# Attention, two-expert routing and an MLP on one core: row sums with a built-in 1e-9, the routing's noise one step later, the first loads reordered

## The chip, the cores and the metric

One core of a Trainium2 chip. The metric is the device time of one execution in microseconds. The kernel before takes 890.91 us, the median of three runs (889.0 to 891.82).

## What is computed

Three parts, one after the other, in fp32.

1. Attention with hashed buckets, for 2 batches of 8 heads with 768 positions of 64 numbers. A query sees only the keys whose six sign bits (of `q @ proj`) are the same as its own:

```python
mask = q_bucket[:, :, :, None] == k_bucket[:, :, None, :]
scores = np.where(mask, scale * q @ k^T, -1e9)
attn = np.exp(scores - max);  attn = attn / (attn.sum(-1) + 1e-9);  out = attn @ v
```

2. A mixture of 8 experts over the 1536 rows of 512 that come out: `noisy = x @ w_gate + log1p(exp(x @ w_noise)) * noise`, the two best experts per row with softmax weights, and for each `relu(x @ w1[e]) @ w2[e]`.
3. An MLP with 2048 inner columns: `h = x @ w_in`, `h * sigmoid(1.702 h) @ w_out`.

## The kernel before, in words

**The attention** (`attention`, L506) is a software pipeline of 96 steps g. One step is 128 queries of one head against all 768 keys. Six steps make a unit u: two heads j and three blocks c of 128 queries; 16 units in all. TensorE is PE in the profile, VectorE DVE, ScalarE ACT, GpSimd POOL; SP issues most DMAs. Each engine works off its instructions in program order, and the order is written out by hand. In step g the program emits:

- `a_score(g+2)` (L288): four matmuls into one of two PSUM tiles `s`; `a_soft(g+2)` on DVE: the row maximum `mx` (L300) and two small operations `sm` (L301, L302);
- `a_trans(g)` (L330): six transposes of `P` into the two PSUM tiles `p`, each half copied to SBUF by ACT or DVE (L259, L265; `copy` picks the one with less work booked so far);
- `a_exp(g+2)` (L311) on ACT: exponentials into `P`, whose row sums go into a small tile `rs` (`accum_out`);
- in some steps `a_av` (L341): `P^T` times `v` into columns 0 to 383 of the PSUM tile `av` (`self.pa`); once per unit its copy `xu`;
- then whatever the table `sched` holds for this step. `at(g, f)` puts a call there; `at_m` does the same for calls that use the one PSUM tile `m`, and moves each to a step that no other such call has.

**Closing a unit** (`a_xt`, L351, 18 calls) stands in that table. It takes the PSUM tile `m` (the last call a tile `p`) of 512 columns. DVE adds 1e-9 to the unit's row sums and writes them into columns 480 to 485 of that same tile (L371), and takes the reciprocal into the SBUF tile `rc` (L372). PE then multiplies `xu` with the gate weights into columns 384 to 479 (L376) and transposes `xu` into columns 0 to 383 (L379). DVE scales both by `rc` (L382, or L384 and L385; and L386).

**The routing** of a quarter of the rows (`r_route`, L400) is cut into small functions, `soft` to `weights`, one per step. `soft` sums the logits into columns 392 and up of the tile `av` (L420 to L422), and has ACT take Exp and Ln (L423, L424). `noisy` (L427 to L429) combines that with the noise; its operands lie in `av` as well. `top` and `index` find the two best experts. For the first two quarters a loop (L567 to L576) gives each function its step. When the slots are known POOL scatters the rows to memory (L485), six DMAs for a quarter; `f_load` (L614) then reads the first expert's rows back, and `f_tr` (L619) transposes them (L821): the mixture begins.

**The start.** `a_load(0)` (L129) issues four loads of 384 KB: q of head 0, q of head 1 and k of head 1 from SP, k of head 0 from ACT. `consts` then issues the 16 KB of `projq` from ACT (L66) and the signs `sgn` from POOL (L72). 40 dummy matmuls (L514) run meanwhile. For the first unit the splitting of q and k into high and low parts is written out: `z_q` (L210) scales q into `u1` and `u2` (L218 or L216, L219) and subtracts (L220); `z_k` (L222) does k (L229 or L227, L230); for head 0 the engines are ACT and DVE, for head 1 POOL takes most. `z_hash` (L232) multiplies q and k with `projq` (L183) and turns the result into sign rows on DVE (L245, four per head) and ACT (L247).

Of the kernel before, what the change touches and what calls it, by code (L numbers as in the profile page):

```python
# [10 lines left out]
F32 = mybir.dt.float32  # L11
# [4 lines left out]
AF = mybir.ActivationFunctionType  # L16
ALU = mybir.AluOpType
AX = mybir.AxisListType
# [3 lines left out]
B, H, S, D = 2, 8, 768, 64  # L22
# [7 lines left out]
HALF = 384  # L30
# [8 lines left out]
SCALE = 1.0 / math.sqrt(D)  # L39


class Kernel:
# [19 lines left out]
    def consts(self):  # L62
        nc, a = self.nc, self.a
        p = self.cpool
        self.projq = self.t(p, [128, 32], F32, "projq")
        nc.scalar.dma_start(self.projq, a["projq"])  # L66
        self.sc = self.t(p, [128, 2], F32, "sc")
        nc.vector.memset(self.sc, 1.0)
        nc.vector.memset(self.sc[0:64, 0:1], SCALE)
        nc.vector.memset(self.sc[64:128, 1:2], SCALE)  # L70
        self.sgn = self.t(p, [128, 1], F32, "sgn")
        nc.gpsimd.dma_start(self.sgn, a["sgn"])  # L72
        self.ident = self.t(p, [128, 128], F32, "ident")
        make_identity(nc, self.ident)
# [39 lines left out]
    def attn_pools(self, ctx):  # L114
        self.ap = self.pool("attn", ctx=ctx, side="right")
        self.ps_s = self.pool("ps_s", 2, PSUM, ctx=ctx)
        self.ps_p = self.pool("ps_p", 2, PSUM, ctx=ctx)
        self.ps_a = self.pool("ps_a", 1, PSUM, ctx=ctx)
        self.ps_m = self.pool("ps_m", 1, PSUM, ctx=ctx)
        self.pa = self.t(self.ps_a, [128, 512], F32, "av")  # L120
        self.iotp = self.pa[:, HALF:HALF + 8]
        self.raw, self.uv, self.vt, self.hb = {}, {}, {}, {}
        self.tail = 0
        self.la = self.ld = 0.0
        self.rt = {}
        self.S, self.P, self.PT, self.AV = {}, {}, {}, {}
        self.RS, self.XR, self.LG, self.sm, self.xu = {}, {}, {}, {}, {}

    def a_load(self, n):  # L129
        nc, a = self.nc, self.a  # L130
        b, p = divmod(n, 4)
        raw = {}
        for j in range(2):
            for nm in ("q", "k"):
                t = self.t(self.ap, [128, S], F32, f"raw{nm}{j}", 1)
                eng = nc.scalar if n == 0 and j == 0 and nm == "k" else nc.sync
                eng.dma_start(t, a[nm + "T"][b, 2 * p + j])
                raw[nm, j] = t
        self.raw[n] = raw

# [69 lines left out]
    def z_q(self, j, hf, eng):  # L210
        nc = self.nc
        u1, v1, u2, v2 = self.uv[0, j]
        cs = slice(hf * HALF, (hf + 1) * HALF)
        q = self.raw[0]["q", j][:, cs]
        if j == 1 and hf == 0:
            eng.tensor_scalar(u1[:, cs], q, self.sc[:, 0:1], None, op0=ALU.mult)  # L216
        else:
            nc.scalar.activation(u1[:, cs], q, AF.Copy, scale=self.sc[:, 0:1])  # L218
        nc.vector.tensor_scalar(u2[0:64, cs], q[0:64, :], SCALE, None, op0=ALU.mult)  # L219
        eng.tensor_tensor(u1[64:128, cs], q[64:128, :], u1[64:128, cs].bitcast(F32), op=ALU.subtract)  # L220

    def z_k(self, j, eng):  # L222
        nc = self.nc
        u1, v1, u2, v2 = self.uv[0, j]
        k = self.raw[0]["k", j]
        if j == 1:
            eng.tensor_scalar(v1, k, self.sc[:, 1:2], None, op0=ALU.mult)  # L227
        else:
            nc.scalar.activation(v1, k, AF.Copy, scale=self.sc[:, 1:2])  # L229
        eng.tensor_tensor(v2[0:64, :], k[0:64, :], v1[0:64, :].bitcast(F32), op=ALU.subtract)  # L230

    def z_hash(self, j):  # L232
# [59 lines left out]
    def a_soft(self, g):  # L292
        nc = self.nc
        u, s, n, qh, j, c = self.dec(g)
        ps = self.S.pop(g)
        if s == 0:
            self.RS[u] = self.t(self.ap, [128, 3, 2], F32, "rs", 4)
        mx = self.t(self.ap, [128, 1], F32, "mx", 4)
        sm = self.t(self.ap, [128, 2], F32, "sm", 4)
        nc.vector.tensor_reduce(mx, ps[:, :, :HALF], axis=AX.XY, op=ALU.max, negate=True)  # L300
        nc.vector.tensor_scalar(sm[:, 0:1], mx, BIG / 2, None, op0=ALU.is_lt)  # L301
        nc.vector.tensor_scalar(sm[:, 1:2], mx, BIG / 2, mx, op0=ALU.is_lt, op1=ALU.mult)  # L302
        self.sm[g] = (sm, ps)
        self.use(dve=1.15)

    def a_exp(self, g):
        nc = self.nc
        u, s, n, qh, j, c = self.dec(g)
        sm, ps = self.sm.pop(g)
        P = self.t(self.ap, [128, 2, HALF], F32, "P", 3)  # L310
        nc.scalar.activation(P, ps[:, :, :HALF], AF.Exp, bias=sm[:, 1:2], scale=sm[:, 0:1],  # L311
                             accum_out=self.RS[u][:, c, j:j + 1])
        self.P[g] = P
        self.use(act=1.08)

# [35 lines left out]
    def a_xt(self, u, c=None, spare=False):  # L351
        nc = self.nc
        n, qh = self.un(u)
        b, p = divmod(n, 4)
        bq = 2 * b + qh
        c0, nch = (0, 3) if c is None else (c, 1)
        xu = self.xu.pop((u, c))
        if p == 0:
            if bq == 0:
                self.pad(self.ap, 96, "pad_xr")  # L360
            if bq in (1, 2):
                self.XR[bq] = self.t(self.x0, [128, 4 * CAP], F32, "xe" + "lh"[bq - 1], 1)[:, :3 * DM].rearrange("p (i d) -> p i d", i=3)
            else:
                self.XR[bq] = self.t(self.ap, [128, 3, DM], F32, "xr", 1)
            if bq == 2:
                self.pad(self.x0, 32, "pad_x0")
            self.LG[bq] = self.t(self.ap, [128, 3, 2, 16], F32, "lg", 3)
        ps = self.t(self.ps_p, [128, 512], F32, "p") if spare else self.mt([128, 512])
        rc = self.t(self.ap, [128, 3, 2], F32, "rc", 1)[:, :nch, :]
        rp = ps[:, 480:486].rearrange("p (c j) -> p c j", j=2)[:, :nch, :]  # L370
        nc.vector.tensor_scalar(rp, self.RS[u][:, c0:c0 + nch, :], 1e-9, None, op0=ALU.add)  # L371
        nc.vector.reciprocal(rc, rp)  # L372
        pt = ps[:, 0:nch * 128].rearrange("p (c d) -> p c d", c=nch)
        pl = ps[:, 384:384 + nch * 32].rearrange("p (c j e) -> p c j e", c=nch, j=2)
        for x in range(nch):
            nc.tensor.matmul(ps[:, 384 + 32 * x:416 + 32 * x], xu[:, x * 128:(x + 1) * 128], self.wg[:, p, :],  # L376
                             start=True, stop=True)
        for x in range(nch):
            nc.tensor.transpose(pt[:, x, :], xu[:, x * 128:(x + 1) * 128], self.ident)  # L379
        lg = self.LG[bq][:, c0:c0 + nch]  # L380
        if p == 0:
            nc.vector.tensor_tensor(lg, pl, rc[:, :, :, None].to_broadcast([128, nch, 2, 16]), op=ALU.mult)  # L382
        else:
            nc.vector.tensor_tensor(pl, pl, rc[:, :, :, None].to_broadcast([128, nch, 2, 16]), op=ALU.mult)  # L384
            nc.vector.tensor_tensor(lg, pl, lg, op=ALU.add)  # L385
        nc.vector.tensor_tensor(  # L386
            self.XR[bq][:, c0:c0 + nch, p * 128:(p + 1) * 128].rearrange("p c (j d) -> p c j d", j=2),
            pt.rearrange("p c (j d) -> p c j d", j=2),
            rc[:, :, :, None].to_broadcast([128, nch, 2, 64]), op=ALU.mult)
        self.use(dve=1.0)  # L390
        if p == 3:
            self.x_store(bq, c0, nch)
# [113 lines left out]
    def attention(self):  # L506
# [3 lines left out]
        nc = self.nc  # L510
        LA = 2
        ps = self.t(self.ps_s, [128, 2, 512], F32, "s")
# [51 lines left out]
        g = 0  # L564
        for bq, sc in ((0, 64), (1, 75)):
            g = max(xt[6 + bq], g) + 1
            self.at(g, self.r_stage, bq, 0, 3)  # L567
            for nm in ("soft", "noisy", "top", "index", "pick"):
                self.at(g, self.r_do, bq, nm)
                g += 1  # L570
            g = self.at_m(g, self.r_do, bq, "rank", "place")
            self.at(g + 1, self.r_do, bq, "slots")
            self.at(g + 2, self.r_do, bq, "weights")
            for i in range(3):
                self.at(max(g + 2, sc) + i, self.r_scatter, bq, i)
            g += 2  # L576
        for g in range(G):
            self.g = g
            u, s, n, qh, j, c = self.dec(g)
# [711 lines left out]
    def run(self):  # L1291
# [12 lines left out]
        with ExitStack() as cw:  # L1304
# [2 lines left out]
            self.x0 = self.pool("x0", ctx=cx, side="right")  # L1307
            self.hp = self.pool("hp", ctx=cx, side="right")
            with ExitStack() as c2:
                self.attn_pools(c2)  # L1310
                self.a_load(0)
                self.consts()
                self.consts2()
                self.attention()
# [60 lines left out]
```

## Time and profile before

| | |
|---|---|
| median of the runs (three) | 890.91 us |
| the profiled execution | 888.24 us |
| its span in the profile | 886.5 us |
| PE busy | 852.6 us, 96% |
| DVE busy | 529.5 us, 60% |
| ACT busy | 441.7 us, 50% |
| POOL busy | 215.5 us, 24% |
| attention, from the start to the first matmul of the mixture | 283.24 us |

The profile is of one execution. The span is the time from its first to its last instruction on the core; the execution's own time has 1.74 us around it. A share of busy time is a mean over the whole span: in the first 283 us DVE, ACT and PE work together, behind them PE works nearly alone.

### The profile page before, as it was taken

Reading aid. Unit: us, or ns where it says so; the run is one execution under the profiler, and the core shown is the slowest. Engines: PE = TensorE matmul, PEld = TensorE weight load, DVE = VectorE, ACT = ScalarE, POOL = GpSimd, SP = SyncE. Lnnn points to the kernel's source line nnn. Section 1 sums busy time; section 2 is a strip of 40 time slices with the busy share of each in tenths; the row PEclk is TensorE's granted clock in tenths of the full one; section 3 lists DMA queues with packets and bytes.
Section 4 is the critical chain, followed back from the end, with each engine's and each line's share of the span. In section 5 each row is a group of like instructions: output and inputs, shape, how many; then the busy total and the mean of one; then the engine's idle time right before and its main releaser. Section 6 shows DMA issues by size and latency. Waiting matters only on the chain.

```text
span 886.5 us, 14086 instructions
## 1 busy us (share of the span) xinstructions
PE 852.6 (96%) x5409; PEld 742.9 (84%) x5409; DVE 529.5 (60%) x1083; ACT 441.7 (50%) x781; POOL 215.5 (24%) x222
## 2 busy tenths in 40 slices
PE   7899999898987999999999999999999999999997
PEld 5667666566666999999999999988889898989897
DVE  7776777876664578989898888738613121213120
ACT  5787888786763354444444354448514141414130
POOL 4231554296011400000000000006615050514040
PEclk7999999999999999999999999999999999999999
DMA  3746644563114757978787686749311101010000
GB/s 95 252 134 207 178 135 125 167 208 86 55 60 167 254 198 227 300 223 275 248 285 251 225 297 205 220 141 325 112 39 28 44 25 49 13 60 1 24 2 26
DMA packets 52088, 132.19 MB, mean 149 GB/s; under 512 B 8880, under 2 KB 10480, under 8 KB 52016
## 3 DMA queue, kind: packets, MB, share of 16 engines
q1 hardware_dynamic: 43200, 108.82, 37.6%
q0 software_dynamic: 6992, 20.37, 7.5%
q10 hardware_dynamic: 1824, 2.05, 0.8%
q8 instruction: 44, 0.72, 0.3%
q14 instruction: 28, 0.23, 0.1%
HBM read 92.05 MB, written 35.39 MB: 144 GB/s over the span
## 4 chain that ended last, share of the span: by engine, by line
PE 84%; DVE 8%; ACT 4%; issue 2%; DMA 1%; ACTq 0%; DVEq 0%
PE av L341 6%; PE s L288 5%; PE y L866 5%; PE y L868 5%; PE y L867 5%; PE h L842 5%; PE h L843 5%; PE h L844 5%; PE g L1100 5%; PE g L1099 5%; PE g L1101 5%; PE p L330 4%; PE o L1147 4%; PE o L1145 4%; PE o L1146 4%; DVE mx L300 3%
## 5 line engine op out<-in xcount | busy, mean ns | idle before, releaser
L311 ACT ACTIVATE P<-s,sm 128x768 f32<-128x768 f32 x96 | 95.2, 992 | 23.0 <-DVE sm L302 19.4
L1109 POOL TENSOR_TENSOR gl<-sg,gh 128x512 fp32r<-128x512 f32 x48 | 65.7, 1368 | 165.1 <-ACT gh L1108 165.1
L300 DVE TENSOR_REDUCE mx<-s 128x1 f32<-128x768 f32 x96 | 91.4, 952 | 23.3 <-PE s L288 22.7
L288 PE MATMUL s<-v,u 76*128 76x384 f32 (+1 forms) x384 | 95.1, 370 | 4.5 <-ACT P L311 2.3
L1054 POOL DMA_INDIRECT yg<-ys,ysl x24 | 24.5, 1020 | 303.3 <-DMA ys<-xel 296.8
L288 PEld LDWEIGHTS s<-v,u 76*128 76x128 f32 (+1 forms) x384 | 64.6, 195 | 30.0 <-issue 11.0
L330 PE MATMUL p<-ident,P 128*128 128x128 f32 x576 | 83.2, 279 | 6.0 <-ACT PT L259 2.9
L1105 DVE TENSOR_TENSOR sg<-g,sg 128x512 f32<-128x512 f32 x48 | 33.2, 691 | 91.9 <-ACT sg L1104 87.5
L330 PEld LDWEIGHTS p<-ident,P 128*128 128x128 f32 x576 | 68.8, 142 | 15.5 <-ACT PT L259 5.2
L341 PE MATMUL av<-PT,v 128*64 128x384 f32 (+1 forms) x216 | 74.7, 476 | 2.2 <-DVE rw L422 1.7
L849 ACT ACTIVATE hh<-h 128x416 fp32r<-128x416 f32 x56 | 29.0, 519 | 72.7 <-PE h L844 72.2
L866 PE MATMUL y<-hh,wh 128*128 128x416 f32 (+1 forms) x144 | 51.1, 355 | 0.0
L868 PE MATMUL y<-hh,wl 128*128 128x416 f32 (+1 forms) x144 | 49.8, 346 | 0.0
L867 PE MATMUL y<-hl,wh 128*128 128x416 f32 (+1 forms) x144 | 49.7, 345 | 0.0
L341 PEld LDWEIGHTS av<-PT,v 128*64 128x64 f32 x216 | 26.2, 142 | 27.4 <-issue 23.4
L1104 ACT ACTIVATE sg<-g 128x512 f32<-128x512 f32 x48 | 28.7, 597 | 39.7 <-PE g L1101 37.3
L1108 ACT ACTIVATE gh<-sg 128x512 fp32r<-128x512 f32 x48 | 30.3, 630 | 32.2 <-DVE sg L1105 31.3
L259 ACT ACTIVATE PT<-p 128x384 f32<-128x384 f32 x75 | 33.3, 486 | 20.0 <-PE p L330 19.8
L1099 PE MATMUL g<-x2h,wh 128*128 128x256 f32 x144 | 40.0, 278 | 1.6 <-DVE sg L1105 1.0
L850 DVE SCALAR_TENSOR_TENSOR hl<-h,hh 128x416 fp32r<-128x416 f32 x56 | 32.9, 588 | 14.2 <-ACT hh L849 14.1
L1100 PE MATMUL g<-x2l,wh 128*128 128x256 f32 x144 | 39.9, 277 | 0.4 <-DVE x2l L1084 0.4
L1100 PE MATMUL g<-btl,wh 128*128 128x256 f32 x144 | 40.2, 279 | 0.0
(334 smaller groups left out, 2550.1 us busy)
## 6 DMA issues: line engine op xcount, KB each, us to landing
ws<-in_w SPq DMA_DIRECT2D x40, 512.0 KB, 4.7
d_in<-in_w SPq DMA_DIRECT2D x32, 512.0 KB, 5.1
bth<-in_w SPq DMA_DIRECT2D x16, 512.0 KB, 4.8
btl<-in_w SPq DMA_DIRECT2D x16, 512.0 KB, 4.5
wd<-d_o SPq DMA_DIRECT2D x32, 256.0 KB, 3.5
xs<-xeh SPq DMA_DIRECT2D x13, 512.0 KB, 7.5
rawq<-in_qT SPq DMA_DIRECT2D x16, 384.0 KB, 4.2
rawk<-in_kT SPq DMA_DIRECT2D x15, 384.0 KB, 4.3
```

What stands on the lines that cost most here:

```text
L288: nc.tensor.matmul(ps[:, hf, :HALF], l[:kk, q0:q0 + 128], r[:kk, hf * HALF:(hf + 1) * HALF], start=st, stop=not st)
L300: nc.vector.tensor_reduce(mx, ps[:, :, :HALF], axis=AX.XY, op=ALU.max, negate=True)
L311: nc.scalar.activation(P, ps[:, :, :HALF], AF.Exp, bias=sm[:, 1:2], scale=sm[:, 0:1], accum_out=self.RS[u][:, c, j:j + 1])
L330: nc.tensor.transpose(ps[:, kb, :], P[:, hf, kb * 128:(kb + 1) * 128], self.ident)
L341: nc.tensor.matmul(self.AV[u, c][64 * j:64 * j + 64, :], self.vt[n][:, kb, 64 * j:64 * j + 64], self.PT[u, j][:, kb, cs], start=(kb == 0), ...
L842: nc.tensor.matmul(ps, wh[:, fs], xh[:, d, :n], start=(d == 0), stop=False)
L866: nc.tensor.matmul(ps, wh[:, ds_], hh[:, f, :], start=(f == 0), stop=False)
L867: nc.tensor.matmul(ps, wh[:, ds_], hl[:, f, :], start=False, stop=False)
L868: nc.tensor.matmul(ps, wl[:, ds_], hh[:, f, :], start=False, stop=(f == 7))
L1099: nc.tensor.matmul(ps[:, x, :], wh[:, fs], xh[:, d, :], start=(d == 0), stop=False)
L1100: nc.tensor.matmul(ps[:, x, :], wh[:, fs], xl[:, d, :], start=False, stop=False)
L1109: nc.gpsimd.tensor_tensor(gl[:, fo, :], g, gh[:, fo, :].bitcast(F32), op=ALU.subtract)
```

## The change

Four edits.

1. The four tiles `rs` get a second column per row sum. They are allocated once, with the pools, and POOL fills them with 1e-9. The exponentials write their sum into the first column. `a_xt` sums the two columns with a `tensor_reduce` into the SBUF tile `rc` and takes the reciprocal in place. The PSUM tile of `a_xt` is 480 columns wide, and DVE no longer writes into it before PE does.
2. For the first two quarters of rows `noisy` moves to the step of `top`; the step that it had is left empty, and everything behind it keeps its step.
3. `projq` is loaded first on ACT's queue, ahead of k of head 0. On SP the first halves (columns 0 to 383) of q of both heads come first, then k of head 1, then the second halves: five loads in place of three.
4. The first half of `u2` of head 0 is scaled by ACT, behind its work on k, and no longer by DVE.

```diff
@@ consts
-        self.projq = self.t(p, [128, 32], F32, "projq")
-        nc.scalar.dma_start(self.projq, a["projq"])
@@ attn_pools
+        self.rsum = [self.t(self.ap, [128, 3, 2, 2], F32, "rs", 4) for _ in range(4)]
+        for r in self.rsum:
+            self.nc.gpsimd.memset(r, 1e-9)
@@ a_load
+        if n == 0:
+            nc.scalar.dma_start(self.projq, a["projq"])
+            raw = {(nm, j): self.t(self.ap, [128, S], F32, f"raw{nm}{j}", 1) for j in range(2) for nm in ("q", "k")}
+            nc.scalar.dma_start(raw["k", 0], a["kT"][b, 2 * p])
+            for nm, j, c0, c1 in (("q", 0, 0, HALF), ("q", 1, 0, HALF), ("k", 1, 0, S), ("q", 0, HALF, S), ("q", 1, HALF, S)):
+                nc.sync.dma_start(raw[nm, j][:, c0:c1], a[nm + "T"][b, 2 * p + j][:, c0:c1])
+            self.raw[n] = raw
+            return
...
-                eng = nc.scalar if n == 0 and j == 0 and nm == "k" else nc.sync
-                eng.dma_start(t, a[nm + "T"][b, 2 * p + j])
+                nc.sync.dma_start(t, a[nm + "T"][b, 2 * p + j])
@@ z_q
-        nc.vector.tensor_scalar(u2[0:64, cs], q[0:64, :], SCALE, None, op0=ALU.mult)
+        if j or hf:
+            nc.vector.tensor_scalar(u2[0:64, cs], q[0:64, :], SCALE, None, op0=ALU.mult)
@@ z_k
             nc.scalar.activation(v1, k, AF.Copy, scale=self.sc[:, 1:2])
+            nc.scalar.activation(u2[0:64, :HALF], self.raw[0]["q", 0][0:64, :HALF], AF.Copy, scale=SCALE)
@@ a_soft, a_exp
-            self.RS[u] = self.t(self.ap, [128, 3, 2], F32, "rs", 4)
+            self.RS[u] = self.rsum[u % 4]
-                             accum_out=self.RS[u][:, c, j:j + 1])
+                             accum_out=self.RS[u][:, c, j, 0:1])
@@ a_xt
-        ps = self.t(self.ps_p, [128, 512], F32, "p") if spare else self.mt([128, 512])
+        ps = self.t(self.ps_p, [128, 480], F32, "p") if spare else self.mt([128, 480])
         rc = self.t(self.ap, [128, 3, 2], F32, "rc", 1)[:, :nch, :]
-        rp = ps[:, 480:486].rearrange("p (c j) -> p c j", j=2)[:, :nch, :]
-        nc.vector.tensor_scalar(rp, self.RS[u][:, c0:c0 + nch, :], 1e-9, None, op0=ALU.add)
-        nc.vector.reciprocal(rc, rp)
+        nc.vector.tensor_reduce(rc, self.RS[u][:, c0:c0 + nch], axis=AX.X, op=ALU.add)
+        nc.vector.reciprocal(rc, rc)
@@ attention
-            for nm in ("soft", "noisy", "top", "index", "pick"):
-                self.at(g, self.r_do, bq, nm)
+            for nm in (("soft",), (), ("noisy", "top"), ("index",), ("pick",)):
+                self.at(g, self.r_do, bq, *nm)
                 g += 1
@@ run
+                self.projq = self.t(self.cpool, [128, 32], F32, "projq")
                 self.attn_pools(c2)
```

## Rows read from the trace of the kernel before

**Rows 1.** Busy time by stretch of the span: each engine's, PE clock, DMA share, GB/s

```profile
22.00:280.00 258.00, 239.32 (x1637) 168.06 (x1635) 180.84 (x521) 192.57 (x384) 102.14 (x112) 0.98 0.47 146
...
300.00:886.50 586.50, 577.83 (x3548) 544.14 (x3546) 323.00 (x480) 229.73 (x362) 94.48 (x80) 1.00 0.46 150
```

**Rows 2.** Waits of PE, 0 to 300 us: total us, times, longest

```profile
PE m L376 <- DVE rc L372: 7.7, 6, 2.5
```

**Rows 3.** Timeline: PE's matmuls of L376 that stood idle first (start, us)

```profile
147.91 0.86 PE L376 MATMUL m<-wg,xu 128*128 128x32 f32 x6 [0.52 <-DVE rc L372]
177.31 0.85 PE L376 MATMUL m<-wg,xu 128*128 128x32 f32 x6 [0.89 <-DVE rc L372]
212.55 0.83 PE L376 MATMUL m<-wg,xu 128*128 128x32 f32 x6 [1.70 <-DVE rc L372]
249.57 0.85 PE L376 MATMUL m<-wg,xu 128*128 128x32 f32 x6 [1.08 <-DVE rc L372]
268.23 0.85 PE L376 MATMUL m<-wg,xu 128*128 128x32 f32 x6 [2.49 <-DVE rc L372]
274.30 0.38 PE L376 MATMUL m<-wg,xu 128*128 128x32 f32 x2 [1.02 <-DVE rc L372]
280.41 0.38 PE L376 MATMUL p<-wg,xu 128*128 128x32 f32 x2 [1.08 <-DVE rc L372]
```

**Rows 4.** Timeline around 66, 178 and 212 us: DVE, POOL and ACT

```profile
66.17 1.81 POOL L174 TENSOR_TENSOR u<-rawq,u 64x768 fp32r<-64x768 f32 x1
...
66.44 0.20 DVE L372 RECIPROCAL rc<-m 128x6 f32<-128x6 f32 x1
...
179.59 0.87 ACT L259 ACTIVATE PT<-p 128x384 f32<-128x384 f32 x2
...
211.55 0.55 DVE L265 COPY PT<-p 128x384 f32<-128x384 f32 x1
```

**Rows 5.** PE alone by stretch: length, PE busy, PE clock, DMA share, GB/s

```profile
214.00:218.00 4.00, 4.00 (x17) 0.57 0.08 16
...
269.00:273.00 4.00, 4.00 (x33) 0.57 0.37 112
```

**Rows 6.** Timeline at the attention's end: SP and PE; a line of the DMA view

```profile
271.12 0.38 SPq L815 DMA_DIRECT2D PT<-xs  x1
...
280.76 1.47 PE L821 MATMUL s<-ident,PT 128*128 128x128 f32 x12
...
PT<-xs SPq DMA_DIRECT2D x1, 768.0 KB, 4.8
```

**Rows 7.** Source lines L371, L372 and L463: duration in ns min/median/max

```profile
L371 DVE TENSOR_SCALAR m<-rs x17: 152/156/158, 50.0 to 276.0; 128x6 f32<-128x6 f32 x15, 128x2 f32<-128x2 f32 x2
...
L372 DVE RECIPROCAL rc<-m x17: 170/196/197, 50.1 to 276.2; 128x6 f32<-128x6 f32 x15, 128x2 f32<-128x2 f32 x2
...
L463 DVE TENSOR_REDUCE slot<-pw x4: 203/203/203, 167.4 to 287.8; 128x6 int32<-128x48 f32 x4
```

**Rows 8.** Timeline of the routing's second quarter: DVE's first of three, and the matmul behind

```profile
179.44 0.18 DVE L427 SCALAR_TENSOR_TENSOR av<-av,rw 128x24 f32<-128x24 f32 x1
...
181.17 0.54 PE L341 MATMUL av<-PT,v 128*64 128x384 f32 x1
```

**Rows 9.** Timeline of the start: DVE and POOL; a line of the DMA view

```profile
6.59 1.25 POOL L216 TENSOR_SCALAR u<-rawq,sc 128x384 fp32r<-128x384 f32 x1 [3.43 <-DMA rawq<-in_qT]
...
8.01 0.61 DVE L245 TENSOR_SCALAR u<-m,sgn 12x384 fp32r<-12x384 f32 x1
...
11.30 1.81 POOL L230 TENSOR_TENSOR v<-rawk,v 64x768 fp32r<-64x768 f32 x1
...
11.76 1.56 DVE L219 TENSOR_SCALAR u<-rawq 64x384 fp32r<-64x384 f32 x1
...
projq<-in_projq ACTq DMA_DIRECT2D x1, 16.0 KB, 5.6
```

**Rows 10.** Source line L219: duration in ns min/median/max, first and last start

```profile
L219 DVE TENSOR_SCALAR u<-rawq x4: 343/349/1561, 5.2 to 18.4; 64x384 fp32r<-64x384 f32 x4
```

## The prediction

> **What bounds the kernel now.** I read the busy time by stretch first. From 300 us to the end PE is busy for 577.83 of 586.5 us at full clock, and nothing that the change touches runs there: that stretch only moves as a whole. From 22 to 280 us PE is busy for 239.32 of 258 us, so 18.7 us are idle, and its clock is 0.98 of full, while DVE has 181 and ACT 193 busy us [rows 1]. PE sets the pace there too, but it is held up now and then; what can be had is those 18.7 us and the clock. The waits of PE come next. The longest is that of the gate matmuls (L376) for the reciprocal (L372), 7.7 us in six times [rows 2]; with a seventh, on the tile `p`, it is 0.52 + 0.89 + 1.70 + 1.08 + 2.49 + 1.02 + 1.08 = 8.78 us, each time starting 0.05 to 0.14 us after a reciprocal's end [rows 3]. PE needs no result of that reciprocal. It waits because DVE works in columns 480 to 485 of the PSUM tile that the matmuls write; the columns differ, so the wait goes by the tile. Third, PE's clock: it is 0.57 of full from 214 to 218 us and from 269 to 273 us [rows 5], each time just behind one of the two longest of these stalls (1.70 and 2.49 us); nowhere else between 50 and 280 us does it fall for long. 0.57 is mostly the lower level, 1.2 GHz.
>
> **Row sums.** Of the pair L371 and L372, 0.156 and 0.196 us [rows 7], the first becomes a reduction of 128x12 to 128x6, the second works in place. The nearest reduction takes 0.203 us [rows 7], so a pair costs 0.00 to 0.05 us more, 18 times, on an engine with 77 us to spare: nothing. Four small memsets on POOL at the start, ahead of the load of `sgn`, cost nothing while POOL waits 3.43 us for q anyway [rows 9]; without that cover, some 0.1 us each.
>
> What counts is the wait. PE is then held only by the copy `xu`, made a step or more earlier, and by the tile `m`, which its last user left a step earlier. I go through the stalls, each in two bounds: nothing (another wait takes over) and the whole stall.
> - 147.91 (0.52): the copies behind it come 0.5 us earlier too, as DVE's scaling moves up with PE. I take 0.45.
> - 177.31 (0.89): the next transposes need ACT's copies, which end at 180.46 [rows 4] and move less than PE. I take 0.6.
> - 212.55 (1.70): the transposes behind need a DVE copy that ends at 212.10 [rows 4], 0.45 us before the old start. Less what is then late, 1.2.
> - 249.57 (1.08): the exponential that PE needs next is ready; 1.0.
> - The clock from 214 to 218: four busy microseconds at 0.57 do 2.28 us of work, so 1.7 us are lost [rows 5]. I take 1.65.
> - The end. From 268.23 on, 2.49, 1.02 and 1.08 us of stalls [rows 3] and another 4 x (1 - 0.57) = 1.7 us of clock [rows 5] are 6.3 us by which PE could reach the transposes of the mixture (L821, 280.76 us) sooner. But these need the first expert's rows, issued at 271.12 us and landed 4.8 us later [rows 6], at 275.9. So only 280.76 - 275.9 = 4.8 us are to be had here, and the wait for that load is late next. The load itself waits for the scatters, which move up with the gains before them.
>
> Sum: 0.45 + 0.6 + 1.2 + 1.0 + 1.65 + 4.8 = 9.7 us. Bounds: 0, and 8.78 + 3.4 = 12.2 us.
>
> **The noise.** Three DVE operations (the first at 179.44, 0.18 us [rows 8], so some 0.6 us in all) leave the place ahead of a row maximum and stand behind the next one, twice. Their operands lie in the tile `av`, so the matmuls of `av` two steps on may now wait for them: in the second quarter those start at 181.17 [rows 8], and the three, moved behind a row maximum and its two small operations, would end close to that. The maximum and so the exponential ahead gain up to 0.6. I take 0; bounds -0.6 and +0.6 us for each of two.
>
> **The start.** `projq` lands 5.6 us after its issue, behind k [rows 9], and was the last thing the first hash matmuls waited for. That wait hides nothing, but behind it DVE is as late: its first sign operation starts at 8.01 [rows 9], when its work on k is done, and that hangs on ACT's copy of k. k of head 0 is now issued second on its queue, yet only half of q is ahead of it on the other; 0.3 us either way. SP issues five loads for three, so the weights, noise and v behind them come two issues later; none is used for tens of microseconds. ACT's extra scaling stands behind the copy of k, before its first work on signs, 0.5 us in a gap. The one size that shows: DVE's second scaling (L219) takes 1.56 us, against 0.35 elsewhere [rows 10]; it begins at 11.76, while POOL works on v (11.30 to 13.11) [rows 9]. POOL began when q of head 1 landed, at 6.59 [rows 9]; its first half is now half the size and ahead, and POOL should be done 1 us or more sooner. Bounds: -0.9 us (the second halves of q come late) and +1.2 us. I take +0.6.
>
> **Sum** 9.7 + 0.6 = 10.3 us off the profiled execution's 888.24, so 877.9. That execution lay 2.7 us below the median; off the median of 890.91 the forecast is 880.6 us.
>
> **A rule on the shared port.** The rows show L219 at 343 to 349 ns, and once at 1561, beside a POOL operation on SBUF [rows 9, 10]. The Trainium skill (SBUF — State Buffer, Who interferes with whom) has a DVE operation in a two-port mode and a GpSimd operation lock each other out, names copies and `tensor_scalar` for it, and says that `tensor_reduce` never contends; the trace agrees for L219. The page does not name the reciprocal; by the rule the new reduction is free, and the sum stays 10.3. What follows if the reciprocal does contend is a rival below.
>
> **Rivals.**
> - *The stall is handed on.* ACT is 75% busy from 22 to 280 us [rows 1] and its exponential releases the score tiles. If PE runs into those releases instead, half of the four stalls in the loop comes back (1.6 of 3.25), the clock still falls at 214, and half of the end is lost to late copies: 1.6 + 0.6 + 2.4 = 4.6 us, 886.3. For it: 177.31 shows such a limit. Against it: DVE's work that feeds ACT moves up by the same time as PE. Chance 0.20.
> - *The wait stays.* The last reader of the tile `m` is DVE too; if the matmul waits for DVE's progress all the same, nothing changes but the start: 890.3. Against it: that reader is a step back in all of rows 3 but the last three. Chance 0.12.
> - *Slower: the reciprocal waits for POOL.* It read PSUM and now reads and writes SBUF, as L219 does. POOL is busy 40% of the stretch [rows 1]. At 66.44 the reciprocal began inside a POOL operation of 1.81 us, with 1.54 us of it left [rows 4]; that is the largest of such overlaps. If each of 18 lost the 1.2 us that L219 lost and row maxima behind it held PE, that is 21.6 us against 10.3: 902.2. It decides when the mean loss that reaches PE passes (10.3 + 2.7) / 18 = 0.72 us. Against it: PE no longer waits for this reciprocal, and most of them fall into gaps of POOL. Chance 0.08.
>
> **How the numbers follow.** The forecast itself has 0.60, from 877.5 (all stalls, the clock and the start: 13.4) to 883.4 (no clock won at 214, nothing from the start, the noise 0.6 against it: 7.5). A measurement of this kernel tells 0.3%, 2.7 us, from no change. The handed-on stall lies beyond that too: faster 0.60 + 0.20 = 0.80; same 0.12; slower 0.08. The range leaves out the last two: 876.5 to 888.0, one microsecond wider below than the bounds for DVE's own freed waits.
>
> **What would show it.** In the profile after: no wait of L376 for L372; L376 right behind the matmuls before it; full clock at 214 to 218 and 269 to 273 us; the first L821 some 10 us earlier, with PE idle before it until the load of the first expert's rows lands; L219 at 0.35 us four times; the stretch behind unchanged in length. Wrong would be: L376 idle with another DVE releaser; new idle time before the scores or transposes of like size; reciprocals of over 1 us; a lower clock in places where it was full.

## The result, and the profile after

The changed kernel takes 880.67 us (median of four runs, 880.10 to 883.22) against 891.37 us (889.00 to 892.96) of the kernel before on the same chip: a ratio of 0.9876, 95% interval 0.9849 to 0.9902. The forecast was 880.6. The profiled execution of the changed kernel took 880.22 us, 8.0 less than the profiled one of before, while the medians lie 10.7 apart. The two numbers have to be explained apart.

Busy time by stretch, of the kernel after (columns as in [rows 1]):

```profile
22.00:272.00 250.00, 235.99 (x1631) 165.82 (x1630) 179.82 (x515) 190.93 (x380) 101.65 (x110) 0.99 0.49 150
292.00:878.50 586.50, 578.24 (x3549) 544.84 (x3547) 322.99 (x480) 230.12 (x362) 96.10 (x80) 1.00 0.46 150
```

The last 586.5 us hold the same PE work as before (578.24 us busy for 577.83): that stretch has only moved. From 22 to 272 us PE is idle for 14.0 of 250 us, for 18.7 of 258 before. Its waits from 0 to 300 us, in the kernel after (total us, times, longest):

```profile
PE s L298 <- ACT P L321: 3.8, 7, 1.2
PE p L340 <- ACT PT L269: 3.2, 5, 1.2
PE p L340 <- DVE hl L275: 2.5, 2, 2.1
PE m L385 <- ACT xu L269: 1.9, 1, 1.9
...
PE av L351 <- DVE rw L431: 1.5, 1, 1.5
```

The wait of [rows 2] is gone: no line has the gate matmuls (L385 now) wait for a reciprocal. They wait once, for `xu`. The timeline of PE at the attention's end, kernel after, against the last rows of [rows 3]:

```profile
260.33 0.75 PE L385 MATMUL m<-wg,xu 128*128 128x32 f32 x6
...
262.96 0.88 PE L340 MATMUL p<-ident,P 128*128 128x128 f32 x6
265.79 0.41 PE L385 MATMUL m<-wg,xu 128*128 128x32 f32 x2 [1.95 <-ACT xu L269]
...
272.63 0.31 PE L388 MATMUL p<-ident,xu 128*128 128x128 f32 x1
272.77 1.47 PE L830 MATMUL s<-ident,PT 128*128 128x128 f32 x12
```

Where 2.49 us were idle (268.23 of before) the six matmuls start at once; 5.5 us later a new stall of 1.95 us stands. PE alone by stretch, kernel after, against [rows 5]:

```profile
210.00:214.00 4.00, 4.00 (x27) 1.00 0.26 53
214.00:218.00 4.00, 3.89 (x25) 1.00 0.19 70
266.00:270.00 4.00, 4.00 (x33) 0.58 0.70 229
```

The clock no longer falls behind 212 us, and still falls at the end, now behind the new stall. The load of the first expert's rows, kernel after, from the timeline of SP and from the DMA view ([rows 6] of before):

```profile
265.85 0.38 SPq L824 DMA_DIRECT2D PT<-xs  x1
```

```profile
PT<-xs SPq DMA_DIRECT2D x1, 768.0 KB, 5.3
```

It lands at 271.15 (265.85 + 5.3), and L830 follows L388 without idle time at 272.77: PE does not wait for it. Three source lines of the kernel after (ns, minimum, median, maximum), against [rows 7] and [rows 10]:

```profile
L380 DVE TENSOR_REDUCE rc<-rs x18: 147/156/159, 48.7 to 273.2; 128x6 f32<-128x12 f32 x15, 128x2 f32<-128x4 f32 x3
...
L381 DVE RECIPROCAL rc<-rc x18: 166/191/192, 48.9 to 273.4; 128x6 f32<-128x6 f32 x15, 128x2 f32<-128x2 f32 x3
...
L228 DVE TENSOR_SCALAR u<-rawq x3: 344/345/871, 11.6 to 17.6; 64x384 fp32r<-64x384 f32 x3
```

The pair costs what it cost; no reciprocal is stretched, though five of the eighteen start while a POOL operation on SBUF runs (the one at 65.00 behind L182, which began at 64.70). DVE's scaling of the start still takes 0.87 us once in place of 0.34, where it took 1.56 and the prediction had 0.35 each time.

To see where the gain arises I read, of every profile, when the exponential of each pipeline step starts. The table gives that start in the first profile of before, and by how much it is earlier (us) in the others; the last lines are the first transposes of the mixture (L821 of before, L830 of after) and the whole span. The four columns on the right are experiments described below; they ran on another chip.

| step | before, first profile | after | before, second profile | before, no early scatters | after, no early scatters | after, scatters spread |
|---|---|---|---|---|---|---|
| 5 | 25.18 | 1.28 | 0.00 | 0.54 | 1.41 | 0.34 |
| 53 | 148.28 | 1.69 | -0.41 | 0.58 | 1.72 | 0.74 |
| 54 | 151.53 | 2.27 | -0.42 | 0.58 | 2.30 | 1.32 |
| 63 | 177.62 | 2.63 | -0.42 | 0.58 | 2.66 | 1.69 |
| 64 | 181.26 | 3.74 | -0.42 | 0.58 | 3.77 | 2.79 |
| 66 | 185.24 | 3.26 | -0.41 | 0.58 | 3.28 | 2.31 |
| 71 | 197.57 | 3.32 | -2.67 | 0.57 | 3.35 | 2.38 |
| 72 | 199.27 | 1.64 | -2.97 | 0.56 | 3.34 | 2.37 |
| 76 | 211.73 | 1.66 | -2.71 | 0.64 | 3.40 | 2.17 |
| 78 | 220.55 | 5.22 | -2.70 | 0.66 | 6.90 | 5.73 |
| 84 | 235.00 | 4.07 | -4.22 | 0.66 | 6.88 | 4.81 |
| 89 | 249.31 | 4.05 | -4.21 | 0.66 | 6.86 | 4.79 |
| 90 | 253.73 | 5.25 | -4.22 | 0.66 | 8.07 | 5.99 |
| 95 | 267.97 | 5.25 | -4.21 | 0.67 | 8.08 | 5.99 |
| mixture | 280.76 | 7.99 | -5.47 | 0.63 | 11.72 | 10.26 |
| span | 886.5 | 8.0 | -7.2 | -1.1 | 9.3 | 7.6 |

In the changed kernel the gain grows in jumps where stalls of [rows 3] stood, and falls twice: by 1.7 us at step 72 and by 1.15 between steps 78 and 84. The first fall is this stall, from the timelines of DVE and PE, kernel after:

```profile
195.68 0.56 DVE L275 COPY hl<-p 128x384 f32<-128x384 f32 x1 [2.65 <-PE s L298]
...
196.29 0.87 PE L340 MATMUL p<-ident,P 128*128 128x128 f32 x6 [2.05 <-DVE hl L275]
```

DVE stands still for 2.65 us ahead of a copy of transposes that began at 191.08, and PE then waits for that copy. No producer in the trace is that late: L298, which it names as the releaser, began at 193.27 and took 0.97 us. The first profile of before has nothing like it at this place.

From the mixture's first transposes to the end the two first profiles take 605.8 and 605.7 us, the four others of the table 607.5, 607.5, 608.1 and 608.4 (in the order of the columns). So 1.7 to 2.7 us of the last line arise behind the attention on that chip, and why is not shown.

### The profile page after: what moved, and what is told of

Same layout as the page of the kernel before. It is cut to its first block, busy times and chain, and to the rows that moved or that the text cites. A ratio compares the mean times of both kernels' runs of the same rounds, so it can differ in the third digit from the quotient of the medians.

```text
span 878.5 us, 14095 instructions
## 1 busy us (share of the span) xinstructions
PE 849.7 (97%) x5409; PEld 740.5 (84%) x5409; DVE 528.2 (60%) x1082; ACT 441.8 (50%) x782; POOL 218.4 (25%) x226
## 3 DMA queue, kind: packets, MB, share of 16 engines
q10 hardware_dynamic: 1824, 2.05, 0.8%
## 4 chain that ended last, share of the span: by engine, by line
PE 87%; DVE 6%; ACT 4%; DMA 1%; issue 1%; another core or an unknown queue 0%; SPq 0%; ACTq 0%; DVEq 0%
PE av L351 7%; PE s L298 6%; PE y L875 5%; PE y L877 5%; PE y L876 5%; PE g L1109 5%; PE g L1108 5%; PE g L1110 5%; PE h L851 5%; PE h L852 5%; PE h L853 5%; PE p L340 5%; PE o L1156 4%; PE o L1154 4%; PE o L1155 4%; DVE mx L310 2%
## 5 line engine op out<-in xcount | busy, mean ns | idle before, releaser
L298 PE MATMUL s<-v,u 76*128 76x384 f32 (+1 forms) x384 | 93.3, 365 | 5.2 <-ACT P L321 3.8
L298 PEld LDWEIGHTS s<-v,u 76*128 76x128 f32 (+1 forms) x384 | 63.0, 191 | 30.5 <-issue 13.0
```

The lines of the kernel that those rows point to most:

```text
L298: nc.tensor.matmul(ps[:, hf, :HALF], l[:kk, q0:q0 + 128], r[:kk, hf * HALF:(hf + 1) * HALF], start=st, stop=not st)
```

## The experiments

Four kernels ran first, each a part of the change on the kernel before (893.35 us on that chip); four on a second chip (before: 893.92), four on a third (895.72). Ratios are each to the kernel before on the same chip.

**Row sums alone.** The kernel before with edit 1.

```diff
-        ps = self.t(self.ps_p, [128, 512], F32, "p") if spare else self.mt([128, 512])
+        ps = self.t(self.ps_p, [128, 480], F32, "p") if spare else self.mt([128, 480])
-        rp = ps[:, 480:486].rearrange("p (c j) -> p c j", j=2)[:, :nch, :]
-        nc.vector.tensor_scalar(rp, self.RS[u][:, c0:c0 + nch, :], 1e-9, None, op0=ALU.add)
-        nc.vector.reciprocal(rc, rp)
+        nc.vector.tensor_reduce(rc, self.RS[u][:, c0:c0 + nch], axis=AX.X, op=ALU.add)
+        nc.vector.reciprocal(rc, rc)
...
```

> The kernel before with the row-sum edit alone: second column of 1e-9, reduction and reciprocal in SBUF, the PSUM tile of 480 columns. Theory (the gate matmuls no longer wait for DVE): 8 to 9 us below the kernel before, ratio about 0.990; no wait of the gate matmuls for a reciprocal in the trace, the stalls of 1.70 and 2.49 us gone, TensorE at full clock from 209 to 216 us. Rival (the start brought most of it): no more than 2 us below, ratio 0.998 or more. Rival (the three edits need each other): neither this nor the other parts alone give over half of the whole.

Measured: 884.57 us, 0.9917 [0.9894, 0.9939], 8.8 us. This one edit holds most of the gain. PE's clock is full from 209 to 216 us. At the end the stall of 2.49 us is gone, but another stands near its place, 2.35 us ahead of the gate matmuls at 270.44, for DVE's scaling of `xr` (L388).

**Row sums in SBUF, same arithmetic.** The kernel before, with only its six columns moved out of the matmuls' tile.

```diff
-        rp = ps[:, 480:486].rearrange("p (c j) -> p c j", j=2)[:, :nch, :]
+        rp = self.t(self.ap, [128, 3, 2], F32, "rp", 1)[:, :nch, :]
```

> The kernel before with one word of the row-sum edit: the sum with 1e-9 is written by the same operation into a small SBUF tile of its own, not into columns 480 to 485 of the PSUM tile; no second column, no reduction, no early tiles. Theory (what counts is that DVE leaves the matmuls' PSUM tile alone): the same gain as the whole row-sum edit, within 1 us of it, 8 to 9 us below the kernel before. Rival (the second column or the once allocated tiles matter): no more than 2 us below.

Measured: 884.59 us, 0.9911 [0.9882, 0.994]. It is the same gain, as far as the intervals tell. The second column of 1e-9 and the reduction do nothing for the time that shows; what counts is that DVE leaves the PSUM tile. The first lines of PE's waits, 0 to 300 us, of this kernel:

```profile
PE p L330 <- ACT PT L259: 5.4, 6, 1.9
PE s L288 <- ACT P L311: 3.5, 8, 0.6
PE m L376 <- ACT xu L259: 2.0, 1, 2.0
```

L376 and the reciprocal are no longer on a line together.

**Loads alone.** The kernel before with edits 3 and 4.

```diff
+            for nm, j, c0, c1 in (("q", 0, 0, HALF), ("q", 1, 0, HALF), ("k", 1, 0, S), ("q", 0, HALF, S), ("q", 1, HALF, S)):
+                nc.sync.dma_start(raw[nm, j][:, c0:c1], a[nm + "T"][b, 2 * p + j][:, c0:c1])
...
```

> The kernel before with the reordered and halved first loads and ACT's scaling of the first half of u2, and nothing else. Theory: the exponentials run 1.3 us ahead of before from step 5 on, as in the changed kernel, and keep about that to the end of the attention: 1 to 1.5 us below the kernel before, ratio about 0.9985. Rival (the start brought most of it): 8 us below, ratio 0.991.

Measured: 894.46 us, 1.0020 [1.0002, 1.0038]: no gain, so the theory missed. Its profile is 1.2 us ahead at step 5, 1.1 at step 66, and 1.2 behind at step 71, at the stall near 195 us that is treated below. PE waits as before:

```profile
PE m L383 <- DVE rc L379: 8.1, 7, 2.5
```

**Noise alone.** The kernel before with edit 2.

```diff
-            for nm in ("soft", "noisy", "top", "index", "pick"):
-                self.at(g, self.r_do, bq, nm)
+            for nm in (("soft",), (), ("noisy", "top"), ("index",), ("pick",)):
+                self.at(g, self.r_do, bq, *nm)
```

> The kernel before with the noise one step later for the first two quarters, and nothing else. Theory: within 1 us of the kernel before, as DVE has gaps at both places; the exponential behind the old place up to 0.6 us earlier, twice. Rival (the noise held DVE ahead of a row maximum and so the whole loop): 1 to 2 us below. Rival (its operands in the tile av now hold the matmuls of av): 0.5 to 1.5 us above, with a wait of those matmuls for the noise in the trace.

Measured: 892.62 us, 0.9991 [0.9976, 1.0006]. In its profile the exponential of step 64 is 0.53 us better placed than that of step 63, and that of step 66 has lost 0.63 again: what the maximum ahead gains, the one behind pays.

**The whole change again**, unaltered.

> The whole change again, unaltered, as the mark for the three beside it. If the gain is a property of the program: a ratio of 0.985 to 0.990 to the kernel before, an execution 9 to 13 us shorter. If what the first profile showed (8.0 us between two single executions, 10.7 us between medians) was the luck of the executions: 0.990 to 0.993. The short stalls at 195 and 223 us, in which PE, ACT and DVE wait on one another without a late producer in the trace, recur in this profile if they belong to the scatters that run there (2 us each, within 3 us of the same place), and are elsewhere or gone if they are chance.

Measured: 883.61 us, 0.9889 [0.9858, 0.9921], 10.3 us. The stall at 195 us came again (DVE idle for 2.77 us until 196.53), and one of 2.38 us at 265.93. The start was slower: 0.92 us gained at step 5, and PE waited longer for the late half of q (the view of PE's waits, 0 to 300 us):

```profile
PE av L191 <- DMA rawq<-in_qT: 2.3, 1, 2.3
```

**Without the noise's move.** The whole change with the five functions one per step, as before.

```diff
-            for nm in (("soft",), (), ("noisy", "top"), ("index",), ("pick",)):
-                self.at(g, self.r_do, bq, *nm)
+            for nm in ("soft", "noisy", "top", "index", "pick"):
+                self.at(g, self.r_do, bq, nm)
```

> The change without the noise's move: row sums with their second column and the reordered start. Theory (noise worth nothing): within 1.2 us of the whole change, the exponential of step 64 only 0.4 to 0.6 us behind it. Rival (the parts reinforce one another: the noise's place decides whether the maximum of the step before is late once the matmuls no longer wait): 3 to 5 us slower than the whole change, as the three parts alone sum to some 6 us only where the whole gains 10.

Measured: 884.21 us, 0.9899 [0.9866, 0.9931]: 0.6 us behind the whole change, within what can be told. The parts do not reinforce one another.

**Without the reordered loads.** The whole change with `a_load`, `z_q` and `z_k` as before.

```diff
-        if n == 0:
-            nc.scalar.dma_start(self.projq, a["projq"])
...
+        self.projq = self.t(p, [128, 32], F32, "projq")
+        nc.scalar.dma_start(self.projq, a["projq"])
```

> The change without the reordered loads: row sums and noise. Theory (the start is worth what it shows at its end, 1.3 us at the fifth exponential, and keeps it): 1 to 2 us slower than the whole change, ratio about 0.990. Rival (the loads alone gained 1.1 us at the start and lost it again further on, so they are worth nothing): the same time as the whole change. Second rival (the parts reinforce one another): 3 us or more slower.

Measured: 882.70 us, 0.9875 [0.9848, 0.9902]: the same as the whole change. So the first rival of that expectation holds for the total, though not by its reason: at step 5 the seven profiles with the reordered loads are 1.28, 1.21, 1.41, 0.92, 0.64, 0.34 and -0.20 us ahead of the first profile of before (mean 0.80), the six others without them -0.62, -0.13, 0.68, -0.14, 0.00 and 0.54 (mean 0.06). Some 0.7 us are there, inside a scatter as wide.

**`soft` one step later.** The whole change, with `soft` moved into the empty step.

```diff
-            for nm in (("soft",), (), ("noisy", "top"), ("index",), ("pick",)):
+            for nm in ((), ("soft",), ("noisy", "top"), ("index",), ("pick",)):
```

> The whole change, with the routing's soft moved one step later for the first two quarters, into the step that the change left empty. After the change PE waits once, 1.5 us, in the second quarter, for a DVE operation of soft's neighbourhood on the tile av. Theory: that wait goes, 0.5 to 1.5 us faster than the whole change. Rival: Exp and Ln of soft now stand on ACT behind a later exponential, and noisy, one step behind, waits for them on DVE ahead of a row maximum: 0 to 2 us slower than the whole change.

Measured: 885.82 us, 0.9908 [0.9876, 0.9939]. The wait for L431 (1.47 us at 172.27 in the kernel after) is gone, and two others stand a little later in the timeline of PE:

```profile
177.28 0.97 PE L298 MATMUL s<-v,u 128*128 128x384 f32 x4 [1.00 <-ACT P L321]
178.85 0.93 PE L340 MATMUL p<-ident,P 128*128 128x128 f32 x6 [0.61 <-ACT PT L269]
```

Against the whole change's second profile its exponentials gain 0.36 us at step 63 and lose 0.37 at step 64. Its profile then lost 1.25 us at steps 72 and 73, at a clock of 0.79 from 196 to 204 us, behind the stall at 197.97 that the other has too (there the clock stayed full). The move earns next to nothing; that it costs 2 us is not shown.

**The kernel before again**, unaltered.

> The kernel before, unaltered, for a second profile of it: the first lay 2.7 us below its median. If the median's surplus sits in stalls like those that the changed kernel shows at 195 and 223 us: this profile, when it lies near the median, shows one or two of about 2 us there, with the exponentials of steps 71 and 80 each 1 to 2 us later than in the first profile, and everything behind 292 us as long as before. If it sits in the clock of the mixture and the MLP: the first matmul of the mixture comes at the same time and the stretch behind is 2 to 3 us longer. Ratio to the kernel before 1.000 within 0.003 by either.

Measured: 896.02 us, 1.0006 [0.998, 1.0032]; its profiled execution took 895.46. The timeline of PE and ACT in this second profile of before:

```profile
195.06 0.55 PE L330 MATMUL p<-ident,P 128*128 128x128 f32 x3
...
197.41 0.49 ACT L259 ACTIVATE PT<-p 128x384 f32<-128x384 f32 x1 [2.39 <-remote]
...
197.95 0.55 PE L330 MATMUL p<-ident,P 128*128 128x128 f32 x3 [2.33 <-issue]
```

PE stops between the third and the fourth of six transposes. The second three write the other of the two tiles `p`, which ACT's copy has to empty first: that copy ends at 197.90, and they start 0.05 us later, although the view names no releaser. So PE waits for ACT. ACT itself is idle for 2.39 us ahead of the copy, with a releaser that the trace names only "remote". POOL ends the sixth of a row of scatters at 197.62. The table shows 2.3 us lost at step 71 and 1.5 more by step 84. So the kernel before has these stalls too, and its first profile was an execution without them.

**Before without early scatters.**

```diff
             for i in range(3):
-                self.at(max(g + 2, sc) + i, self.r_scatter, bq, i)
+                pass
```

> The kernel before without the scatters of the first two quarters of rows (twelve indirect DMAs; the rows that they would bring are not in the mixture's input, and the rest of the work is the same). If these bursts stall the engines in most executions of the kernel before: 2 to 4 us faster, ratio 0.995 to 0.998, and no stall over 1.5 us at 195 to 199 and 223 to 229 us other than those of the gate matmuls. If the stalls belong to something else: the same time within 1 us.

Measured: 890.62 us, 0.9950 [0.9926, 0.9973], 5.1 us faster, more than the 2 to 4 expected, and no such stall in its profile. PE alone at the two places:

```profile
193.00:199.00 6.00, 5.95 (x47) 1.00 0.19 77
221.00:229.00 8.00, 8.00 (x56) 1.00 0.17 50
```

The stalls belong to the bursts of scatters.

**After without early scatters.** The same edit on the changed kernel.

> The changed kernel without the scatters of the first two quarters of rows (twelve indirect DMAs; the rows that they would bring are not in the mixture's input, and the rest of the work is the same). If the scatters' bursts cause the stalls of about 2 us at 195 us and the one at 223: both are gone, the exponential of step 72 keeps the gain that step 66 has (3.3 us in the first profile of the changed kernel, where 72 has 1.6), and the whole is 2 to 4 us faster than the changed kernel. If they are the price of a wait among PE, ACT and DVE that the earlier matmuls brought: the stall at 195 stays within 0.5 us and the time within 1 us.

Measured: 880.70 us, 0.9848 [0.9815, 0.9882]. Both falls of the table are gone: 3.28 at step 66 is 3.34 at step 72, and 6.90 at step 78 is 6.88 at step 84. Its busy time from 193 to 197 us (columns as in [rows 1]) and PE's timeline at the end:

```profile
193.00:197.00 4.00, 3.96 (x31) 2.12 (x30) 2.00 (x5) 4.00 (x9) 2.36 (x1) 1.00 0.02 4
```

```profile
263.59 0.41 PE L385 MATMUL m<-wg,xu 128*128 128x32 f32 x2 [2.58 <-ACT xu L269]
...
269.04 1.47 PE L830 MATMUL s<-ident,PT 128*128 128x128 f32 x12
```

At 195 us PE is busy all the time. That the whole is faster than the changed kernel is not shown: its interval overlaps with the changed kernel's, measured on other chips. The stall at the end stays; the third quarter's scatters, which this kernel keeps, run just ahead of it (POOL ends the sixth at 261.88). It looks like the one at 195 us: copies on ACT and DVE stand still, and the trace names no producer.

```profile
263.26 0.28 ACT L269 ACTIVATE xu<-av 128x128 f32<-128x128 f32 x1 [2.29 <-remote]
263.36 0.56 DVE L275 COPY PT<-p 128x384 f32<-128x384 f32 x1 [2.10 <-remote]
```

In all nine profiles of kernels with the row sums out of the tile, ACT or DVE stands still here for 1.7 to 2.5 us and goes on 1.3 to 1.5 us after the end of the third quarter's sixth scatter. So the end probably pays for a burst as well; no run leaves these scatters out.

**Scatters spread.** The whole change, pairs of scatters three steps apart.

```diff
-                self.at(max(g + 2, sc) + i, self.r_scatter, bq, i)
+                self.at(max(g + 2, sc) + 3 * i, self.r_scatter, bq, i)
```

> The whole change, with the scatters of the first two quarters three steps apart (two DMAs in each of steps 64, 67, 70 and 75, 78, 81) in place of one step. If it is the burst of six that stalls the engines, with the DMA engines at over 400 GB/s: no stall at 195 us, 1 to 3 us faster than the changed kernel, which would make it the fastest of all. If each scatter costs the same wherever it stands, or the stall follows the last of them: the same time, with the stall some 6 to 10 us later.

Measured: 881.42 us, 0.9858 [0.9823, 0.9892], 0.7 us above the kernel without the scatters on the same chip. The stall at 195 us is gone (2.38 at step 71, 2.37 at step 72), most of the one at 223 stays (5.73 at step 78, 4.81 at step 84). On POOL the edit spread only the first quarter, in a row of four and one of two; the second quarter's six still ran in one row, as in the kernel after:

```profile
192.04 0.96 POOL L494 DMA_INDIRECT xs<-xr,slot  x1 [0.22 <-issue]
...
197.54 0.99 POOL L494 DMA_INDIRECT xs<-xr,slot  x1 [0.16 <-issue]
...
214.56 1.05 POOL L494 DMA_INDIRECT xs<-xel,slot  x1 [0.17 <-POOL spacer L493]
215.91 0.98 POOL L494 DMA_INDIRECT xs<-xel,slot  x1 [0.22 <-issue]
...
220.98 0.96 POOL L494 DMA_INDIRECT xs<-xel,slot  x1 [0.22 <-issue]
```

So within one kernel the broken row has no stall and the whole row has one. Compare 194 to 196 us, first in this kernel, then in the kernel after; engines as in [rows 1]:

```profile
194.00:196.00 2.00, 2.00 (x13) 1.44 (x12) 1.62 (x5) 2.00 (x3) 0.99 (x1) 1.00 1.04 420
```

```profile
194.00:196.00 2.00, 0.24 (x2) 0.00 (x0) 0.32 (x1) 1.32 (x3) 1.97 (x2) 1.00 1.04 416
```

The DMA engines are as busy in both (1.04, 420 and 416 GB/s), yet PE is busy for 2.00 us in the one and 0.24 in the other. So traffic as such does not stall the engines. What also differs is the share of the scatters' queue (q0). The DMA view of the same two microseconds, spread first, then the kernel after (packets, MB, share of 16 engines):

```profile
q0 software_dynamic: 200, 0.68, 83.0%
q1 hardware_dynamic: 52, 0.15, 18.4%
```

```profile
q0 software_dynamic: 246, 0.81, 99.3%
...
q1 hardware_dynamic: 4, 0.01, 1.1%
```

But that share does not decide. From 196 to 198 us the first profile of before has as high a share, and PE is busy all the time; its second profile has a lower one, and PE stands still. First the first profile, then the second (the stretch as above, and the queue from the DMA view):

```profile
196.00:198.00 2.00, 2.00 (x15) 1.30 (x10) 1.18 (x5) 2.00 (x5) 1.58 (x2) 1.00 1.02 414
...
q0 software_dynamic: 238, 0.79, 97.6%
```

```profile
196.00:198.00 2.00, 0.05 (x1) 0.05 (x1) 0.00 (x0) 0.59 (x2) 1.40 (x3) 1.00 1.03 417
...
q0 software_dynamic: 197, 0.67, 81.9%
```

Whether this version is faster than the whole change is not settled: 0.9858 here, 0.9876 and 0.9889 there, on other chips, with intervals that overlap.

## Why the prediction was right

**The bound and its cause** held. PE was held by DVE's work in the tile, not by the values: the kernel that moves six columns and nothing else has a ratio of 0.9911, some 8 us.

**The terms** are best read where neither kernel has the scatters' stalls: the difference of the two columns "no early scatters", step by step.

| term | forecast | measured | where |
|---|---|---|---|
| start | 0.6 | 0.87 | step 5 |
| 147.91 | 0.45 | 0.58 | 53 to 54 |
| (not named) | 0 | 0.36 | 54 to 63 |
| 177.31 with the noise | 0.6 | 0.62 | 63 to 66: 1.11, then -0.49 |
| 212.55 and the clock behind | 1.2 + 1.65 | 3.48 | 76 to 78 |
| 249.57 | 1.0 | 1.20 | 89 to 90 |
| the end | 4.8 | 3.68 | 95 to the mixture |
| to the mixture | 10.3 | 11.1 | |
| span | 10.3 | 10.4 | 887.6 to 877.2 |

The rows add up to 10.8; the other 0.3 arises between steps 5 and 53. The medians of this pair, 890.62 and 880.70, differ by 9.9 us. The working was right in its mechanism and its total. Each named term of the loop came out as forecast or up to a third larger: the forecast let copies take some of each stall, and but for 177.31 they took almost none. That the forecast of 880.6 met the median of 880.67 within 0.1 us is luck: the errors of the terms cancelled.

**The end was mis-sized**, and by a wrong step. The prediction capped it at 4.8 us, by the landing of the first expert's rows, and said that PE would be idle until then. In the kernel after, it brought 2.74 us, and the load had landed 1.6 us before L830. What was late next was the copy `xu` on ACT: 1.95 us of new stall, and 4 us at a clock of 0.58 behind it, which give 1.7 us back. Full clock from 269 on was wrong too. In the kernel without early scatters the load (issued at 263.75, 5.2 us to landing) landed at 268.95 and L830 started at 269.04, right behind its predecessor: there both limits came at the same time, so the cap lies where the prediction put it, but it was not the first limit in the kernel after. The stall of 1.95 us stands where the third quarter's scatters end (the last at 263.97; ACT goes on at 265.46, its releaser "remote"), so what the prediction left out at the end is probably again a burst of scatters. That is not tested.

**The reference was a lucky execution.** The sum was made against a profile 2.7 us below the median, and the offset was carried along as if it were noise of no place. Part of it has a place: the second profile of before loses 3.8 us (2.3 and 1.5) at the two bursts of scatters, and the first lost nothing there (without early scatters its exponentials come 0.56 to 0.67 us earlier all the way from step 53 to 95). The rest of the 7.2 us between these two profiles lies elsewhere: 0.4 before step 53, 1.3 at the end of the attention, 1.7 behind it; and the second ran on a chip where the median is 4.4 us higher. The changed kernel's own profile loses 1.7 + 1.15 = 2.8 us there, which is why the two first profiles differ by only 8.0 us: 8.0 + 2.8 = 10.8. Where executions of either kernel pay for these stalls, they drop out of the difference of the medians, which came out at 10.7. That this offset cancelled was not foreseen; the prediction knew nothing of the stalls.

**The rivals.** Handed on: not in the loop; at the end a new stall took the place of the old, probably the scatters'. The wait stays: no. The reciprocal that waits for POOL: no, 166 to 192 ns eighteen times, five of them beside a POOL operation on SBUF. The rule cited ahead, of the Trainium skill (SBUF — State Buffer, Who interferes with whom), that `tensor_reduce` never contends, agrees with L380 at 147 to 159 ns. The noise was worth nothing, as taken, within 0.6 us. The start brought 0.6 to 1.3 us at its end in most profiles, and none that the total shows.

## What to carry to other kernels

In this kernel a scratch column in an accumulator tile made the whole tile a dependency: before a matmul is said to wait for a value, see whether it reads that value at all, and move the scratch to SBUF if it doesn't. A stall that ends in a clock fall can be worth more than its length (1.70 us of idle time brought 3.48). One profile is one execution: where it lies off the median, find the place of the difference in a second profile before the sum is made against it.

## What the runs showed of the hardware

- Around the end of a row of six indirect scatters from POOL's queue PE, ACT and DVE stood still for 1.6 to 3.0 us (the kernel after at 195 us: DVE 2.65, PE 2.05, ACT 1.55; the second profile of before: ACT 2.39, PE 2.33, DVE 3.04), in both kernels, not in every execution. In these two profiles a copy on DVE or ACT stands still first, and PE waits for it. Four and then two in a row did not do it, at the same 420 GB/s, and neither the traffic nor the queue's share decides. How a scatter reaches an engine that touches none of its data stays open. Instruction packets were a candidate: the Trainium skill (Runtime: NRT & Kernel Launch, Instruction fetch mechanics) has each engine fetch its instructions in blocks of 16 KiB by a DMA queue of its own, mostly hidden. The DMA view by single microseconds speaks against it as the sole cause: such a packet fell at 195 us in the kernel after, with the stall, and also at 195 us with the spread scatters, at 426 GB/s, without one; in the second profile of before it came at 200, after PE had gone on.
- The length of a stall does not alone decide whether the clock falls. Behind 1.95 us of idle time at 265.79 the kernel after ran at 0.58. Behind 2.58 us at 263.59 the kernel without early scatters stayed at full clock, 2.4 GHz, and so did the spread kernel behind 1.96 us at 265.05:

```profile
264.00:268.00 4.00, 3.62 (x55) 1.00 0.73 219
```

```profile
265.00:269.00 4.00, 3.57 (x49) 1.00 0.65 194
```
